# A pooled-attention and gated-convolution kernel rewritten: loads of q, token order and the order of work

## The chip, the cores and the metric

The kernel runs on one core of a Trainium2 chip. The metric is the device time of one execution in microseconds (us). The core has five engines that run in order, each its own list: PE (matmul), DVE (vector), ACT (scalar), POOL (GpSimd, which here issues all casting loads) and SP (SyncE, which here issues stores and DMA transposes). They meet through semaphores. Matmul results lie in PSUM, all else in SBUF.

## The reference

Eight batches, eight heads, 576 tokens, head width 64. Keys and values are averaged over groups of eight tokens; attention runs over these 72; its output goes through a gated block.

```python
k_p = k.reshape(B, H, 72, 8, D).mean(axis=3)      # v_p the same
scores = scale * np.matmul(q, k_p.transpose(0, 1, 3, 2))
attn = softmax(scores)
x = matmul(attn, v_p)                            # [B, 576, heads * 64 = 512]
h = np.maximum(x @ w_in, 0.0)                     # 512 -> 1024
conv_out = sum over k in 0..2 of conv_w[k] * h shifted by k-1 tokens
gate = 1 / (1 + exp(-conv_out))
return (h * gate) @ w_out                          # 1024 -> 512
```

q, k, v are normal draws times 0.1, all in float32; the kernel works in bfloat16 with float32 sums.

## The kernel before, in words

Each piece of work is an operation with a name, an engine, inputs and outputs. A list scheduler in the kernel (`Planner`, numbers in `PARAMS["prio"]`) puts them in one order when the program is built; each engine gets its part of it. Where a copy may run on two engines, `PARAMS["act"]` lists the names that go to ACT and the rest go to DVE. Filler matmuls on a tile of zeros (L388) are put where the scheduler expects PE to wait in its first 60 us.

Per batch b the work is:

- `ldk`, `ldv`, `ldq`: loads by POOL, cast to bf16 (L447, L451, L467, L479, L424, L412). All go through POOL's one in-order list.
- Pooling of k and v: three adds on DVE (L605, L612, then L622 for `ksum` or L654 for `vs`). `kT` transposes `ksum` on PE, `kz` copies it into a zero-padded tile.
- q for batches 0 to 4: loaded as [72 rows, heads, 8 tokens x 64], two buffers `q_b`; `qg` regroups it on DVE or ACT into `q2` (L432); 32 PE transposes of 72 columns (`qT`, L688) and copies `qTe` (L694) bring it to `qT`. Its tokens are then in an order of (token mod 8, row). q for batches 5 to 7: five loads of rows of 64 elements (L412) and five DMA transposes by SP (L676) from the same buffer.
- `sc` (scores, L717 and L719): five blocks, each 512 and 64 columns; `exp` on ACT (L725) writes `attnT`. `av` (L742, L746) gives the output and the row sums for 128 tokens (64 for the last tile); `rc` and `nm` on DVE (L755, L759) normalise into `xx`.
- `xt`: `xx` is transposed to `xT` on PE against a permutation matrix `perm` that puts the tokens back in order (L779, copy L785), or by DMA for batches 5 to 7 (L772).
- `mm1` (L799 in two token parts for batch 0, L822 for the others) and `relu` on ACT (L806, L828) give `hT`, eight blocks of 128 channels.
- The convolution: for the (batch, block) pairs in `PARAMS["off"]` two scaled copies (`cp0`, `cp2`, L868 on ACT, L870 on DVE) and two adds (`ca0`, `ca2`, L877, L887) on DVE; for the others six matmuls on PE against diagonal matrices `dw` (`conv`, L945), which POOL builds (L571). `off` holds 54 of 64.
- The gate on ACT (`tanh`, L895 or L952): a sigmoid, or a tanh whose half-plus-half step `tg1` then runs on DVE (L923). A sigmoid needs another function table than exp: a table load before it and one back. Then `g` on DVE (L933) multiplies by h into `gT`.
- `mm2` (L976) per pair of batches, nine row tiles of 128, copies `oe` (L999, L989) and stores by SP (L1004, L994).

w_in is one casting load of 1 MB out of 2 MB (L485), w_out two.

```python
QG = {True: [(0, 8), (8, 16), (16, 24), (24, 32)], False: [(0, 11), (11, 22), (22, 32)]}
"rg": "DDDDDTTT",     # D: regroup and PE transposes; T: small rows and DMA transposes
```

Of the kernel before, what the change touches and what calls it, by code (L numbers as in the profile page):

```python
# [1098 lines left out]
```

## Time and profile before

| | |
|---|---|
| runs, us | 202.21, 202.72, 206.47; median 202.72 |
| profiled execution: span, us | 205.9 |
| PE, DVE, ACT, POOL busy | 95%, 84%, 80%, 28% of the span |
| mean granted TensorE clock | 0.990 |
| DMA: packets, MB | 52,330, 30.02 |

The profiled execution has no other time than its span, the time from its first to its last instruction; it is a separate execution from the three runs. PE's busy share counts filler matmuls (239 of 1770). Engines are listed with the line of the kernel and the tile written and read; a group's mean is the length of one instruction from start to end, which overlaps with the next on the same engine by some 0.1 us. POOL and SP mostly issue transfers, and a transfer's own time is in the DMA rows.

### The profile page before, as it was taken

How to read it: one execution, taken by the hardware profiler on the slowest of the kernel's cores; microseconds unless marked ns; L12 is line 12 of the kernel's file. 1: busy time of each engine (PE TensorE's matmuls, PEld its weight loads, DVE VectorE, ACT ScalarE, POOL GpSimd, SP SyncE). 2: the span in 40 equal slices, each digit the busy share in tenths (PEclk: the TensorE clock that was granted, in tenths of full speed). 3: DMA queues.
4: the chain of work that ended last, by engine and by line, in shares of the span. 5: the costliest groups of instructions: out<-in, count | busy, mean ns of one | idle time of the engine just before them, and what ended most of it. 6: DMA issues, size and time to landing. Idle time of an engine off the chain costs nothing.

```text
span 205.9 us, 4566 instructions
## 1 busy us (share of the span) xinstructions
PE 194.9 (95%) x1770; PEld 133.0 (65%) x1770; DVE 173.3 (84%) x396; ACT 165.3 (80%) x275; POOL 57.0 (28%) x90
## 2 busy tenths in 40 slices
PE   6999999999999999999999999669999999999992
PEld 6978775977557776567755775226756765765541
DVE  3598599999999999999999996893897999778522
ACT  2045799999999999999999999494899867979610
POOL 7999497160223276215412000000000000000000
PEclk9999999999999999999999999996999999999999
DMA  3999999999999999999999999772122625004334
GB/s 32 192 202 205 196 200 200 201 184 192 157 193 238 171 125 173 181 147 158 193 137 167 152 103 151 115 203 105 20 57 41 229 78 155 13 0 168 126 117 154
DMA packets 52330, 30.02 MB, mean 146 GB/s; under 512 B 33468, under 2 KB 47316, under 8 KB 52308
## 3 DMA queue, kind: packets, MB, share of 16 engines
q0 software_dynamic: 32384, 16.73, 71.8%
q1 hardware_dynamic: 19924, 12.99, 30.5%
q8 instruction: 14, 0.23, 0.6%
q14 instruction: 8, 0.07, 0.2%
HBM read 33.44 MB, written 9.44 MB: 208 GB/s over the span
## 4 chain that ended last, share of the span: by engine, by line
PE 38%; DMA 26%; ACT 16%; DVE 12%; issue 3%; POOL 3%; SPq 0%; POOLq 0%; DVEq 0%; ACTq 0%
PE psfB L976 14%; DMA v_b<-in_v_dram 13%; PE psfA L822 12%; DMA q_b<-in_q_dram 6%; DMA qT<-q 6%; ACT tg L895 4%; PE pswA L388 3%; ACT attnT L725 3%; PE psfA L742 2%; ACT hT L828 2%; ACT cv L868 2%; PE psfA L945 2%; DVE p L605 2%; DVE cv L870 1%; DMA xT<-xx 1%
## 5 line engine op out<-in xcount | busy, mean ns | idle before, releaser
L976 PE MATMUL psfB<-w_out,gT 128*128 128x512 bf16 (+1 forms) x282 | 65.4, 378 | 0.0
L822 PE MATMUL psfA<-xT,w_in 128*128 128x288 bf16 x448 | 60.0, 291 | 2.2 <-DMA xT<-xx 2.2
L822 PEld LDWEIGHTS <-w_in 128*128 128x128 bf16 x448 | 43.9, 100 | 16.2 <-DMA xT<-xx 2.4
L976 PEld LDWEIGHTS <-gT 128*128 128x128 bf16 x290 | 27.3, 98 | 28.9
L828 ACT ACTIVATE hT<-psfA 128x576 bf16<-128x576 f32 x56 | 35.1, 656 | 8.4 <-PE psfA L822 8.2
L870 DVE TENSOR_SCALAR cv<-hT,cr 128x576 bf16<-128x576 bf16 x75 | 26.3, 378 | 5.6 <-ACT hT L828 5.4
L933 DVE TENSOR_TENSOR gT<-tg,hT 128x1152 bf16<-128x1152 bf16 x32 | 23.6, 749 | 3.9 <-ACT tg L895 2.0
L759 DVE TENSOR_TENSOR xx<-psfA,rr 128x512 bf16<-128x512 f32 (+1 forms) x40 | 26.5, 679 | 0.2
L868 ACT ACTIVATE cv<-hT,cr 128x576 bf16<-128x576 bf16 x33 | 25.1, 776 | 0.4 <-DVE cv L887 0.2
L725 ACT ACTIVATE attnT<-psfA 128x576 bf16<-128x576 f32 x40 | 24.5, 661 | 0.7 <-PE psfA L717 0.5
L895 ACT ACTIVATE tg<-cv,cn 128x576 bf16<-128x576 bf16 x30 | 22.5, 780 | 0.0
L877 DVE TENSOR_TENSOR cv<-cv,hT 128x1152 bf16<-128x1152 bf16 (+1 forms) x31 | 20.9, 676 | 0.3
L887 DVE TENSOR_TENSOR cv<-cv 128x1152 bf16<-128x1152 bf16 (+1 forms) x31 | 20.8, 674 | 0.2
L999 ACT COPY osb<-psfB 128x512 f32<-128x512 f32 x24 | 14.1, 587 | 6.4 <-PE psfB L976 6.3
L412 POOL DMA_DIRECT2D q<-in_q_dram x15 | 12.8, 863 | 20.1 <-DMA qT<-q 11.3
L895 ACT ACTIVATE tg<-cv,cs 128x576 bf16<-128x576 bf16 x24 | 18.2, 772 | 0.2
L388 PEld LDWEIGHTS <-zero 128*128 128x128 bf16 x239 | 16.1, 108 | 2.8 <-DVE zero L497 2.0
L742 PE MATMUL psfA<-vblk,attnT 128*128 128x130 bf16 (+1 forms) x160 | 15.6, 222 | 2.1 <-DVE xx L759 2.0
L742 PEld LDWEIGHTS <-attnT 128*128 128x128 bf16 (+1 forms) x160 | 11.1, 100 | 5.7 <-DVE xx L759 2.9
L388 PE MATMUL pswA<-zero 128*128 128x128 bf16 x150 | 11.5, 249 | 2.0 <-DVE zero L497 2.0
L717 PE MATMUL psfA<-qT,kz 128*128 128x512 bf16 x64 | 12.4, 286 | 0.3
L746 PE MATMUL psfA<-vblk,attnT 128*128 128x130 bf16 (+1 forms) x80 | 11.2, 221 | 0.0
(92 smaller groups left out, 256.6 us busy)
## 6 DMA issues: line engine op xcount, KB each, us to landing
out_dram<-osb SPq DMA_DIRECT2D x14, 512.0 KB, 4.2
k_b<-in_k_dram POOLq DMA_DIRECT2D x8, 512.0 KB, 13.5
v_b<-in_v_dram POOLq DMA_DIRECT2D x7, 512.0 KB, 13.0
q_b<-in_q_dram POOLq DMA_DIRECT2D x4, 576.0 KB, 15.6
out_dram<-osb SPq DMA_DIRECT2D x7, 256.0 KB, 2.2
q<-in_q_dram POOLq DMA_DIRECT2D x12, 128.0 KB, 15.9
w_in<-in_moe_w_in_dram POOLq DMA_DIRECT2D x1, 1024.0 KB, 10.4
w_out<-in_moe_w_out_dram POOLq DMA_DIRECT2D x2, 512.0 KB, 12.5
```

The lines of the kernel that those rows point to most:

```text
L388: nc.tensor.matmul(out=t, lhsT=zero[:, 0:P], rhs=zero[:, 0:P], start=True, stop=True)
L725: nc.scalar.activation(out=attnT[m][:, t, :], in_=slot(key).rearrange("p i x -> p (i x)")[:, 0:S], func=ACT.Exp, scale=1.0 / 64.0)
L742: nc.tensor.matmul(out=a[0:n, g, c * w:(c + 2) * w], lhsT=attnT[m][:, s, u0:u0 + n], rhs=vblk[m][:, 2 * s:2 * s + 2, :].rearrange("p x d - ...
L759: nc.vector.tensor_tensor(out=xx[i3][0:n].rearrange("p (g h e) -> p g h e", g=2, h=4), in0=av_view()[:, :, :, 0:D], in1=rr[i3][0:n].rearra ...
L822: nc.tensor.matmul(out=t[:, i, 0:HC], lhsT=w_in[:, c, f * P:(f + 1) * P], rhs=xT[m][:, c, i * HC:(i + 1) * HC], start=(c == 0), stop=(c == ...
L828: nc.scalar.activation(out=h_(b)[:, f, hs(b), 2:S + 2].rearrange("p (i x) -> p i x", i=2), in_=slot(key)[:, :, 0:HC], func=ACT.Relu)
L868: nc.scalar.activation(out=cv[y][:, kk // 2, z0:z1, :], in_=src, func=ACT.Copy, scale=sc)
L870: nc.vector.tensor_scalar(out=cv[y][:, kk // 2, z0:z1, :], in0=src, scalar1=sc, scalar2=None, op0=OP.mult)
L877: nc.vector.tensor_tensor(out=cv[y][:, 0, 0:n, :], in0=cv[y][:, 0, 0:n, :], in1=h_at(2), op=OP.add)
L895: nc.scalar.activation(out=tg[i3][:, zs[z0]:zs[z0] + z1 - z0, :], in_=cv[y][:, 0, z0:z1, :], func=ACT.Tanh if half else ACT.Sigmoid, scale ...
L933: nc.vector.tensor_tensor(out=o_, in0=tg[i3], in1=h2, op=OP.mult)
L976: nc.tensor.matmul(out=a[:, 0, j0:j1], lhsT=g[:, c, t * P:(t + 1) * P], rhs=w_out[:, c, j0:j1], start=(c == 0), stop=(c == n_fb - 1), skip ...
```

## The change

The kernel is written anew in these parts; the mathematics stays.

- The scheduler is gone. `PARAMS["order"]` lists all operations in one order, with the PSUM slot of each and the fillers (`14A0/77@B1` means 14 fillers in slot A0 ahead of operation 77).
- q is loaded for every batch as [96 rows, 8 heads, 6 tokens x 64], one buffer `q_b` (batch 0 in rows 0 to 64 and 64 to 96). Batches 0 and 1 (`qp`) skip the regrouping: PE transposes each 64-wide half head by head, 48 instructions (96 for batch 0, in two row ranges). Batches 2 to 4 regroup into one of two `q2` and take 24 transposes of 96 columns. Batches 5 to 7 regroup and take two DMA transposes each.
- Batch 0's scores and exps are in two token ranges, 384 and 192.
- exp writes `attnT` in token order, reading PSUM in steps; `xt` transposes against the identity, and `perm` is gone.
- The last tiles of `av`, `nm` and `xt` are 128 rows high; `attnT` has 64 spare columns of ones.
- Half of w_in comes over SP as float32 into `wf`, SP's first instruction, and four copies `wc` cast it (one on ACT, three on DVE); the other half is cast by POOL's DMA.
- k and v of batch 1 are pooled by eight matmuls each (`pmk`, `pmv`); the other batches pool in place.
- `dw` is built on ACT and DVE. `off` holds 57 of 64: PE keeps blocks 1, 3, 5, 7 of batch 0 and 2, 4, 6 of batch 7.
- All gates are tanh, so all 32 pairs have the `tg1` step, and exp and tanh share one table.

```diff
-        for x, (r0, r1) in enumerate(((0, 64), (64, PR)) if PARAMS["qs"][b] else ((0, PR),)):
-                nc.gpsimd.dma_start(out=q_b[b % NQ][r0:r1].rearrange("p h i d -> p h (i d)"), in_=rows_q(b)[r0:r1])
+            nc.gpsimd.dma_start(out=q_b[b % NQ], in_=q[b].rearrange("h (p i) d -> p h (i d)", i=TQ))
...
-                    nc.sync.dma_start(out=flat_q(m)[:, :, P * t:P * t + n], in_=q_rows(b % NQ)[0:n, t], transpose=True)
+                    nc.sync.dma_start(out=flat_out[:, 1152 * j:1152 * j + 1152].rearrange("p (g r) -> p g r", r=PQ), in_=flat_in[:, 1536 * j:1536 * j + 1536], transpose=True)
...
+                        for z in range(2):
+                            nc.tensor.transpose(out=t[64 * z:64 * z + 64, 0, j * PQ:(j + 1) * PQ], in_=q_b[b % NQ][:, 2 * c + z, i * D:(i + 1) * D], identity=ident[0:PQ, 0:PQ])
...
-            nc.scalar.activation(out=attnT[m][:, t, :], in_=slot(key).rearrange("p i x -> p (i x)")[:, 0:S], func=ACT.Exp, scale=1.0 / 64.0)
+            nc.scalar.activation(out=at(m)[:, t, :].rearrange("p (r i j) -> p r i j", i=2, j=3),
+                                 in_=slot(key)[:, :, 0:HC].rearrange("p i (j r) -> p r i j", j=3), func=ACT.Exp, scale=1.0 / 64.0)
...
-                nc.tensor.transpose(out=a[:, 0, c * P:c * P + n], in_=xx[i3][0:n, c * P:(c + 1) * P], identity=(ident[0:n, 0:n] if tr else perm4 if last else perm))
+                nc.tensor.transpose(out=a[:, 0, c * P:(c + 1) * P], in_=xx[i3][:, c * P:(c + 1) * P], identity=ident)
...
+                nc.sync.dma_start(out=wf, in_=moe_w_in.rearrange("(c p) f -> p c f", p=P)[:, :, 0:512])
+                    copy_on(e)(out=w_in[:, c, 0:512], in_=wf[:, c, :])
...
+                for i in range(8):
+                    nc.tensor.matmul(out=t, lhsT=ident, rhs=src[:, :, i * D:(i + 1) * D], start=i == 0, stop=i == 7)
...
-                    nc.gpsimd.tensor_scalar(out=dw[f][:, kk, :], in0=ident, scalar1=s, scalar2=1.0, op0=OP.mult, op1=OP.mult)
+                    if e == "ACT":
+                        nc.scalar.activation(out=dw[f][:, kk, :], in_=ident, func=ACT.Copy, scale=s)
+                    else:
+                        nc.vector.tensor_scalar(out=dw[f][:, kk, :], in0=ident, scalar1=s, scalar2=None, op0=OP.mult)
...
-    "off": [(0, 2, 3, 6, 7), (0, 3, 4, 6, 7), (0, 1, 2, 3, 5, 6, 7), (0, 1, 2, 3, 4, 5, 6, 7), (0, 1, 2, 3, 4, 5, 6, 7), (0, 1, 2, 3, 4, 5, 6, 7), (0, 1, 2, 3, 4, 5, 6, 7), (0, 1, 3, 5, 7)],
-    "sw": [0, 1, 0, 0, 1, 0, 0, 1],
+    "off": [[0, 2, 4, 6], [0, 1, 2, 3, 4, 5, 6, 7], [0, 1, 2, 3, 4, 5, 6, 7], [0, 1, 2, 3, 4, 5, 6, 7], [0, 1, 2, 3, 4, 5, 6, 7], [0, 1, 2, 3, 4, 5, 6, 7], [0, 1, 2, 3, 4, 5, 6, 7], [0, 1, 3, 5, 7]],
```

The new order on POOL begins with the last part of k, 32 rows of q, k, pieces of v and of the next k, then 64 rows of q; the second batch's k is pooled on PE ahead of the first `mm1`.

More of the change, by code (lines that the diff above doesn't have):

```diff
@@ L286, in packets @@
-def packets(n, nbytes, cast=True, engines=16):
-    return n / engines, 0.003 + 0.0000785 * nbytes if cast else 0.004 + 0.000034 * nbytes, engines // 4
+        out, seen = [], set()
+        for x in PARAMS["order"].split():
+            warm = None
+            if "/" in x:
+                w, x = x.split("/")
+                warm = (int(w[:-2]), w[-2:])
+            mode = x.endswith("s")
+            x, _, slot = x.rstrip("s").partition("@")
+            o = self.ops[int(x)]
+            o.mode = mode
+            assert o.i not in seen and seen.issuperset(o.deps) and (o.after is None or o.after in seen), o.name
+            seen.add(o.i)
+            if slot:
+                self.held[o.take] = (slot[0], int(slot[1]))
+            e = next(iter(o.eng)) if len(o.eng) == 1 else "ACT" if o.name in self.on_act else "DVE"
+            out.append((e, o, warm))
@@ L290 @@
+        assert len(out) == len(self.ops)
+        return out
 @with_exitstack
@@ L438, in load_k, with regroup, fn @@
+    def regroup(b):
+        if QP[b]:
+            return
+        for j in range(2):
+            def fn(e, j=j):
+                copy_on(e)(out=q2[b % NR][:, 3 * j:3 * j + 3], in_=q_b[b % NQ][:, :, 192 * j:192 * j + 192].rearrange("p h (i d) -> p i h d", d=D))
+            pl.add(f"qg.{b}.{j}", {"DVE": 0.48, "ACT": 1.37}, 0, fn, reads=[("ql", b % NQ, 0), ("ql", b % NQ, 1)], writes=[("q2", b % NR, j)])
+    def load_k(b):
         m = b % 2
         src = rows(k, b)
-        acc = PARAMS["acc"][b]
@@ L783, in fn @@
+        pl.add(f"xt.{b}.{t}", "PE", 0.222, fn, reads=[("xx", i3), "ident"], writes=[("xtp", b, t)], take=key2, free=[("xT", m, t)])
         def fn(e):
-            w = 64 if last else P
-            copy_on(e)(out=xT[m][:, :, 128 * t:128 * t + w],
-                       in_=slot(key2)[:, 0, 0:512].rearrange("p (c a) -> p c a", c=4)[:, :, 0:w])
-        pl.add(f"xte.{b}.{t}", {"ACT": 0.48, "DVE": 0.335} if not last else {"ACT": 0.265, "DVE": 0.205}, 0, fn, reads=[("xtp", b, t)], writes=[("xT", m, t)],
-               prio=pr + 0.3, give=key2)
```

824 lines of the change are left out of this document (335 added, 489 removed), and 116 rows, old and new, of the table PARAMS.

## The prediction

> **What bounds the kernel now.** I read the page first (shares and slices), then the busy time by stage, then the chain that ended last, and at its longest transfers the timelines of PE, VectorE and GpSimd.
>
> ```profile
> span 205.9 us, 4566 instructions
> PE 194.9 (95%) x1770; PEld 133.0 (65%) x1770; DVE 173.3 (84%) x396; ACT 165.3 (80%) x275; POOL 57.0 (28%) x90
> PEclk9999999999999999999999999996999999999999
> 0.00:5.00 5.00, 3.00 (x29) 3.00 (x30) 1.76 (x7) 1.28 (x1) 3.78 (x10) 1.00 0.35 28
> 5.00:22.24 17.24, 16.91 (x264) 15.01 (x263) 14.06 (x38) 6.11 (x11) 16.48 (x34) 1.00 1.20 200
> 22.24:44.08 21.84, 21.22 (x274) 16.45 (x271) 19.43 (x48) 20.21 (x39) 11.98 (x17) 1.00 1.26 197
> 44.08:120.00 75.92, 75.75 (x683) 51.34 (x681) 74.43 (x172) 74.87 (x125) 24.79 (x32) 1.00 1.60 169
> 120.00:139.22 19.22, 15.01 (x116) 8.16 (x114) 16.47 (x38) 16.09 (x29) 0.00 (x0) 1.00 1.05 146
> 139.22:202.30 63.08, 63.01 (x419) 39.03 (x419) 46.69 (x96) 46.40 (x74) 0.00 (x0) 0.97 0.30 94
> ```
>
> The columns of a stage are its length, then the busy time of PE, weight loads, DVE, ACT and POOL, the granted clock, the DMA share and GB/s. Five stages differ. To 22.24 us PE waits for batch 0 (much of its busy time there is filler matmuls on `zero`), while from 5 us on the DMA moves 200 GB/s without a pause. From 22.24 to 44.08 batch 1's attention still leaves gaps. From 44.08 to 120 PE, DVE and ACT are all full: 75.75, 74.43 and 74.87 of 75.92 us. From 120 to 139.22 PE idles 19.22 - 15.01 = 4.2 us. Behind it PE alone is full. So the page's 95% hides a start, a stage with three bounds, one stall, and a tail that PE sets.
>
> The stall:
>
> ```profile
> 108.03 0.71 POOL L479 DMA_DIRECT2D v_b<-in_v_dram  x1 [1.92 <-DMA q<-in_q_dram]
> 108.03 21.40 DMA v_b<-in_v_dram
> 129.53 0.83 DVE L605 TENSOR_TENSOR p<-v_b 128x1280 bf16<-128x1280 bf16 x1 [2.50 <-DMA v_b<-in_v_dram]
> 131.36 0.42 PE L742 MATMUL psfA<-vblk,attnT 128*64 128x130 bf16 x4 [2.02 <-DVE xx L759]
> 120.25 1.14 PE L822 MATMUL psfA<-xT,w_in 128*128 128x288 bf16 x8
> 121.23 1.89 PE L976 MATMUL psfB<-w_out,gT 128*128 128x512 bf16 x8
> 139.22 6.62 PE L822 MATMUL psfA<-xT,w_in 128*128 128x288 bf16 x39 [2.19 <-DMA xT<-xx]
> 145.68 0.40 PE L742 MATMUL psfA<-vblk,attnT 128*128 128x130 bf16 x4
> ```
>
> The last tail of v is issued at 108.03 behind loads of q and lands 21.4 us later; DVE, in order, sits before it to 129.53, so batch 5's normalisation, its DMA transposes and mm1 of batch 5 are late. After the gap the clock is low: 39 matmuls take 145.68 - 139.22 = 6.46 us, where 8 take 121.23 - 120.25 = 0.98, so 39 take 4.78. That is 1.7 us more. The stall costs 4.2 + 1.7 = 5.9 us.
>
> **The change part by part.**
>
> *Loads of q.* Batches 5 to 7 take q by 15 loads of 64-element rows and 15 DMA transposes; afterwards every batch has one load of 96 rows (six tokens, 384 elements each; batch 0 has two) and batches 5 to 7 two transposes each.
>
> ```profile
> q0 software_dynamic: 32384, 16.73, 71.8%
> DMA packets 52330, 30.02 MB, mean 146 GB/s; under 512 B 33468, under 2 KB 47316, under 8 KB 52308
> L412 POOL DMA_DIRECT2D q<-in_q_dram x15 | 12.8, 863 | 20.1 <-DMA qT<-q 11.3 <-PE psbB L688 4.4 <-DMA q<-in_q_dram 3.8
> q<-in_q_dram POOLq DMA_DIRECT2D x12, 128.0 KB, 15.9
> ```
>
> One batch had 8 x 576 rows, 4608 small packets; three batches make 13,824 of the 33,468 under 512 B. They become 3 x 768 larger ones. POOL loses 12 issues (nine q issues against 21) and the 20.1 us in which it stood before those loads, eleven of them because the q buffer was still being transposed. Its in-order queue then reaches the last v far sooner than 108.03. I take the whole stall away: -5.9 us. Bounds: 0 if another load is as late (q_b is now single, so each q load waits until the one before is regrouped, and k and v loads stand behind it), -5.9 if none is.
>
> *Start.* Half of w_in goes over SyncE as the first transfer; q of batch 0 goes to PE without VectorE's regrouping; scores and exp come in two token ranges (384 and 192).
>
> ```profile
> 8.79 0.84 DVE L605 TENSOR_TENSOR p<-k_b 128x1280 bf16<-128x1280 bf16 x1 [0.16 <-DMA k_b<-in_k_dram]
> 11.78 0.80 ACT L642 COPY kz<-psbB 64x288 bf16<-64x288 bf16 x2 [7.42 <-PE psbB L636]
> 14.68 2.98 ACT L725 ACTIVATE attnT<-psfA 128x576 bf16<-128x576 f32 x5 [0.48 <-PE psfA L717]
> 17.88 0.40 PE L742 MATMUL psfA<-vblk,attnT 128*128 128x130 bf16 x4
> 22.24 0.81 PE L799 MATMUL psfB<-xT,w_in 128*128 128x384 bf16 x4
> L806 ACT ACTIVATE hT<-psfA 128x384 bf16<-128x384 f32 x5 | 2.5, 492 | 0.4 <-PE psfA L799 0.2
> L806 ACT ACTIVATE hT<-psfA 128x192 bf16<-128x192 f32 x3 | 1.0, 332 | 0.0
> L694 ACT COPY qT<-psbB 128x792 bf16<-128x792 bf16 x4 | 3.3, 814 | 0.0
> ```
>
> K is summed from 8.79 and kz is ready at 12.58. 32 rows of q now go ahead of k instead of 8; that is 0.13 MB more in bf16, 0.65 us at 200 GB/s, so kz is ready at about 13.1 us. Then ACT has four short exps, one copy of q and five long ones. Five exps of 576 took 2.98 us, one lasts 0.66, so they follow each other every 0.58; 0.11 us off each mean above for that overlap gives 4 x 0.22 + 0.70 + 5 x 0.38 = 3.5 us, and AV starts at 16.6 instead of 17.88. From there to mm1 I keep the 22.24 - 17.88 = 4.36 us (three normalisations in order on DVE), giving 21.0: -1.3 us. Best case -3 (k not held up, shorter copies). Worst case +1.5: if the half of w_in (1 MB read, as much as a casting load of 0.52 MB reads, so 2.6 us at 200 GB/s) came wholly ahead of k, the chain would be 2.6 us later, 23.6. The PE list has batch 1's k sum (`pmk.1`, eight matmuls of 320 columns, between eight of 288, 0.98 us, and eight of 512) ahead of the first mm1; that k is behind k, q, v and another k, 2.9 MB of bf16 with itself, 14.5 us from 5 us on, so 19.5 us, and about 1.1 us of matmuls end at 20.6, just inside 21.0.
>
> The first half of w_in is cheap because of the row of the first 5 us: 28 GB/s there against 200 later, so 1 MB put there displaces little. The Trainium skill (DMA: Bandwidth & Descriptors, section "Issuing engines are not separate DMA queues") says that transfers issued from different engines share the same DMA engines, and that this saves issue time alone. By that rule alone the start would be the worst case above, +1.5, and the time 2.8 us longer, 199.3, still in the forecast's own range; that the first 5 us are quiet is why I don't take it, and no run here shows it yet.
>
> *Batch 1 and the PE list.*
>
> ```profile
> L388 PE MATMUL pswB<-zero 128*128 128x128 bf16 x49 | 3.7, 219 | 0.0
> 27.80 0.52 PE L688 MATMUL psbA<-ident,q 72*128 72x72 bf16 x11
> 28.15 0.49 PE L688 MATMUL psbB<-ident,q 72*128 72x72 bf16 x10
> L870 DVE TENSOR_SCALAR cv<-hT,cr 128x576 bf16<-128x576 bf16 x75 | 26.3, 378 | 5.6 <-ACT hT L828 5.4
> L868 ACT ACTIVATE cv<-hT,cr 128x576 bf16<-128x576 bf16 x33 | 25.1, 776 | 0.4 <-DVE cv L887 0.2
> L923 DVE TENSOR_SCALAR tg<-tg 128x1152 bf16<-128x1152 bf16 x11 | 4.9, 446 | 0.4 <-ACT tg L895 0.4
> L923 DVE TENSOR_SCALAR tg<-tg 128x576 bf16<-128x576 bf16 x6 | 1.9, 321 | 0.3 <-ACT tg L952 0.3
> L895 ACT ACT_TABLE_LOAD x3 | 3.8, 1283 | 0.1
> L725 ACT ACT_TABLE_LOAD x2 | 2.6, 1283 | 0.0
> ```
>
> From 34 to 44 us PE ran 49 filler matmuls, 3.7 us. The new list keeps 31 there (13 and 18), about 2.3 us, so 1.4 less; one more convolution (six matmuls at 0.1225 = 0.7) and pmv (1.1) come into that stage, three transposes of q (1.1) leave it: +0.7 + 1.1 - 1.1 - 1.4 = -0.7 us. Bounds: +1.3 if batch 1's 48 half-height transposes do not run in pairs (48 x 0.042 = 2.0 instead of 1.0) and the fillers save nothing; -1.8 if no filler was needed. Later, four convolutions leave PE (10 to 7 in all, one more in batch 0): 4 x 0.74 = 3.0 us off; eleven transposes of 72 columns take 28.15 - 27.80 = 0.35 us, so 32 take 1.0, and 24 of 96 columns take the same if the time goes with the columns; but batch 2's now falls into this part: +1 us. PE -2.0, bounds 0 (DVE and ACT hold it) and -3.
>
> *ACT and DVE.* Without sigmoid five table loads go, 6.4 us of ACT. What comes: every pair now gets the half-plus-half step on DVE, 32 of 1152 columns for 11 and 6 half ones, 32 x 0.446 - 6.8 = +7.5 us; copies scaled on ACT go from 33 to 50, +13.2, on DVE from 75 to 64, -4.2; one more add pair +1.4. ACT takes 12 and DVE 9 of the `dw` builds that POOL made, which lie before 13 us where ACT is idle (6.11 busy of 17.24). Regrouping, pooling in place and copies of q roughly cancel. So ACT has 13.2 - 6.4 = 6.8 us more and DVE 7.5 - 4.2 + 1.4 = 4.7. Batches 1 to 4 and with them about six tenths fall into 44 to 120: 4.1 and 2.8, less the idle 1.05 and 1.5 there, 3.0 and 1.3. The engines work in parallel, so I charge the larger, +3.0 us; 0 if PE stays the bound, +6 if every added microsecond of ACT ends on the path.
>
> *Exp in token order.* It now reads PSUM with a step of 96 elements, three at a time. No row has such a read. Lower bound: the 0.66 us of the row at 14.68. Upper: a second step per element. From 384 to 192 columns the mean falls 492 - 332 = 160 ns, 0.83 ns per element, so 576 x 0.83 = 0.48 us more. I take nothing, since a reciprocal over 8 PSUM values 65 apart costs as little as one over 8 in a row:
>
> ```profile
> L755 DVE RECIPROCAL rr<-psfA 128x8 f32<-128x8 f32 x32 | 5.8, 194 | 1.0 <-PE psfA L746 0.7
> L544 DVE RECIPROCAL cn<-cn 128x8 f32<-128x8 f32 x1 | 0.2, 191 | 0.0
> ```
>
> *Sum*, against the profiled 205.9: -5.9 -1.3 -0.7 -2.0 +3.0 = -6.9, so 199.0 as a span. The runs (202.21, 202.72, 206.47) are 3.2 below the span in the median. If that is one offset, 195.8 comes out; if the shorter runs only had less of the stall, which the change can't save twice, 199.0. A transfer's landing is what differs most easily between executions, but the stall's waits alone would have to shrink from 5.9 to 2.7; I go a quarter of the way from 195.8 to 199.0: **196.5 us**.
>
> **The rivals.**
>
> 1. *DVE and ACT become the bound* (44 to 120 is full already). For: 1.05 and 1.5 us idle. Against: PE's order moves matmuls of mm2 into such gaps. All +6 instead of +3.0, and no gain on PE (+2.0): 196.5 + 5 = 201.5.
> 2. *The stall comes back elsewhere*: single q_b, late v. For: 20.1 us of POOL waits show how an in-order queue passes a late buffer on. Against: 13,824 packets fewer. Without the -5.9 of the stall, but with the half of it that short runs may lack: 196.5 + 4 = 200.5.
> 3. *Slower: exp's strided read costs a second step.* 20 exps of batches 1 to 4 add 20 x 0.48 = 9.6 us to ACT where 1.05 is idle, batch 0 adds 2.4 to the chain at the start; batches 5 to 7 hide in ACT's idle 16.7 us of the tail. 196.5 + 11 = 207.5. It decides from 0.27 us more per exp, 0.93 us mean (then 202.7). Beside it: the Trainium skill (PSUM — Partial Sum Buffer, section "Specifications (TRN2)") says that any non-contiguous pattern slows matmuls significantly, for 8-byte lines; it names matmuls, not ACT's reads, and the two reciprocals do not show it.
>
> **How the numbers follow.** Forecast 0.60, rival 1 0.16, rival 2 0.12, rival 3 0.12. The forecast's own range is 192 to 200: above, 199.0 and a little of the start's bad end; below, the start's good end (-1.7), batch 1's (-1.1) and half of the charge for DVE and ACT (-1.5). For eight in ten it is stretched to **191 to 204**, over rivals 1 and 2, leaving rival 3 out. A change under 2% can't be told from none here: faster means below 198.7, slower above 206.8. Faster: 0.60 x 0.93 + 0.28 x 0.25 = 0.63; slower 0.10, nearly all of rival 3; 0.27 between.
>
> **What would show it.** First mm1 of batch 0 at 20 to 22 us, mm1 of batch 1 before 43. No wait of DVE for v above 1 us, PE idle under 1 us between 120 and 140, clock 9 in all later slices. Loads of q landing in under 10 us. ACT exps of 576 near 660 ns: above 900 rival 3 is right. DVE and ACT over 98% busy with PE idle between 44 and 120: rival 1. A DVE or PE wait of some us for DMA anywhere: rival 2. The forecast is wrong if mm1 starts after 23 us or PE idles more than 5 us behind 44.

## The result: 5.9% slower, and where the time went

| | before | after |
|---|---|---|
| time, us, median | 202.53 | 213.72 (213.12 to 214.95) |
| span of the profiled execution, us | 205.9 | 211.9 |
| ratio after to before, 95% interval | | 1.0585 (1.0517 to 1.0654) |

The forecast was 196.5. In every run of this study that has both numbers the time is the span plus 1.66 to 1.89 us, so the profiled 205.9 of the kernel before stands for some 207.6: it was one of its long executions, 5 us above the median. A second profiled execution of the same kernel had a span of 201.8 and a time of 203.47. The comparisons below go against that one, called the ordinary execution. The ratios compare only executions within 1.5% of the fastest of their kernel: the kernel before also has longer ones, of 204 to 208 us, and where it was run beside the kernel with direct transposes (below) they were 8 of 13, so that over all executions the direct transposes' median, 206.18, is 0.9% above the median of before, 204.43, and not the 1.8% of its ratio.

The page of the kernel after, and its busy time in four of the stages that the prediction used (length, then PE, weight loads, DVE, ACT, POOL, clock, DMA share, GB/s):

```profile
span 211.9 us, 4546 instructions
PE 192.2 (91%) x1752; PEld 130.9 (62%) x1767; DVE 177.7 (84%) x407; ACT 174.4 (82%) x307; POOL 37.4 (18%) x65
PEclk9999999999999999999997599999999999999999
```

```profile
0.00:5.00 5.00, 3.00 (x31) 3.00 (x32) 1.76 (x7) 1.28 (x1) 3.89 (x11) 1.00 0.54 180
5.00:22.24 17.24, 13.07 (x262) 11.14 (x260) 10.74 (x40) 9.84 (x27) 13.14 (x27) 1.00 1.19 183
...
44.08:120.00 75.92, 67.49 (x584) 44.82 (x587) 70.08 (x150) 66.96 (x115) 13.29 (x18) 0.96 1.07 158
120.00:139.22 19.22, 18.43 (x168) 13.03 (x169) 18.34 (x44) 18.38 (x32) 0.00 (x0) 0.98 0.58 129
```

The stall of the stage from 120 us is gone, as forecast: PE is idle for 0.8 us there. But the stage ahead of it, which had 0.2 us idle, now has 8.4, with the clock at 0.96 and a dip to 5 tenths in the page's row. Two of the prediction's own signs of being wrong are there: more than 5 us of idle PE behind 44, and a first mm1 after 23 us (24.92, below). To see how far each kernel is at a given time, take the first relu of a batch as a milestone. First the kernel after, then the ordinary execution of the kernel before, both from the timeline of ACT, for batches 1, 3 and 4:

```profile
47.47 0.63 ACT L709 ACTIVATE hT<-psfA 128x576 bf16<-128x576 f32 x1
99.84 0.65 ACT L709 ACTIVATE hT<-psfA 128x576 bf16<-128x576 f32 x1
128.53 0.64 ACT L709 ACTIVATE hT<-psfA 128x576 bf16<-128x576 f32 x1
```

```profile
45.76 0.67 ACT L828 ACTIVATE hT<-psfA 128x576 bf16<-128x576 f32 x1
95.00 0.65 ACT L828 ACTIVATE hT<-psfA 128x576 bf16<-128x576 f32 x1
114.57 0.65 ACT L828 ACTIVATE hT<-psfA 128x576 bf16<-128x576 f32 x1
```

The differences of these starts, and the rest up to the end of the span, give a table that all experiments are read by:

| profiled execution | to batch 1 | 1 to 3 | 3 to 4 | 4 to end | span |
|---|---|---|---|---|---|
| before, ordinary | 45.76 | 49.24 | 19.57 | 87.23 | 201.8 |
| after | 47.47 | 52.37 | 28.69 | 83.37 | 211.9 |
| two q buffers | 48.84 | 52.40 | 24.67 | 83.09 | 209.0 |
| and later v sum | 48.72 | 52.39 | 21.79 | 83.30 | 206.2 |
| and direct q for batches 2 to 4 | 47.00 | 50.91 | 21.83 | 83.36 | 203.1 |

After against before: +1.7, +3.1, +9.1 and -3.9 us. The largest loss, in the third column, is a wait. The kernel after from 97 to 116 us, from the timelines of POOL, SP, DVE, ACT and PE:

```profile
97.55 0.94 DVE L269 COPY q<-q_b 96x1536 bf16<-96x1536 bf16 x1
...
98.56 15.56 SPq L544 DMA_TRANSPOSE qT<-q  x2
...
98.79 0.78 POOL L261 DMA_DIRECT2D q_b<-in_q_dram  x1 [0.15 <-issue]
...
111.81 0.95 DVE L269 COPY q<-q_b 96x1536 bf16<-96x1536 bf16 x1 [4.13 <-DMA q_b<-in_q_dram]
...
111.85 1.47 ACT L269 COPY q<-q_b 96x1536 bf16<-96x1536 bf16 x1 [5.09 <-issue]
...
113.41 0.40 PE L659 MATMUL psbA<-ident,xx 128*128 128x128 bf16 x4 [3.58 <-DVE xx L641]
115.18 3.57 PE L838 MATMUL psfB<-w_out,gT 128*128 128x512 bf16 x8 [1.38 <-ACT osb L861]
```

Batch 5's last regrouping frees the only q_b at 98.49 and POOL issues batch 6's load at 98.79. In the same moment SP starts the two DMA transposes of batch 5's q, and the load is usable 13 us later. The regrouping of batch 6 stands in the middle of batch 4's normalisation on DVE and of the convolution copies on ACT, so both stop, PE idles 3.58 and 1.38 us, and then eight matmuls of 512 columns take 3.57 us instead of 1.89 (the granted clock from 115 to 119 us is 0.50).

The start, from the timelines of PE and DVE, then the load of k and the DMA rate from the view of the DMA queues over the first 12 us (40 slices of 0.3 us):

```profile
8.76 0.93 PE L532 MATMUL psbB<-ident,q_b 32*64 32x32 bf16 x48 [2.46 <-DMA q_b<-in_q_dram]
...
11.34 0.82 DVE L421 TENSOR_TENSOR k_b<-k_b 128x1280 bf16<-128x1280 bf16 x1
...
24.92 1.46 PE L688 MATMUL psfB<-xT,w_in 128*128 128x384 bf16 x8
```

```profile
GB/s 0 0 0 0 0 0 55 0 7 225 403 389 410 423 416 389 410 379 226 196 197 177 163 149 166 202 182 109 102 116 147 198 195 196 185 201 195 206 202 205
...
k_b<-in_k_dram POOLq DMA_DIRECT2D x1, 512.0 KB, 8.7
```

The last line gives the 512 KB of k 8.7 us from its issue, at 2.57, to its landing. From 3.0 to 5.4 us the DMA moves about 400 GB/s, which is the half of w_in; q is there at 8.76 and k's first sum starts at 11.34 instead of 8.79.

### The profile page after: what moved, and what is told of

Same layout as the page of the kernel before. It is cut to its first block, busy times and chain, and to the rows that moved or that the text cites. A ratio compares the mean times of both kernels' runs of the same rounds, so it can differ in the third digit from the quotient of the medians.

```text
span 211.9 us, 4546 instructions
## 1 busy us (share of the span) xinstructions
PE 192.2 (91%) x1752; PEld 130.9 (62%) x1767; DVE 177.7 (84%) x407; ACT 174.4 (82%) x307; POOL 37.4 (18%) x65
## 2 busy tenths in 40 slices
DMA packets 40987, 30.55 MB, mean 144 GB/s; under 512 B 18348, under 2 KB 35972, under 8 KB 40964
## 4 chain that ended last, share of the span: by engine, by line
PE 57%; DVE 16%; issue 13%; DMA 7%; ACT 3%; POOL 2%; ACTq 0%; POOLq 0%
PE psfB L838 20%; PE psfA L703 15%; DMA q_b<-in_q_dram 7%; PE pswA L237 3%; PE psfB L688 3%; PE psfA L624 3%; PE psfA L808 3%; DVE xx L641 2%; PE psfA L598 2%; PE psbB L659 2%; DVE q L269 1%; ACT attnT L587 1%; DVE cv L746 1%; PE psfA L628 1%; DVE cv L739 1%
## 5 line engine op out<-in xcount | busy, mean ns | idle before, releaser
L759 ACT ACTIVATE tg<-cv,cs 128x576 bf16<-128x576 bf16 x57 | 43.4, 789 | 1.5 <-DVE cv L751 1.5
L737 ACT ACTIVATE cv<-hT,cr 128x576 bf16<-128x576 bf16 x50 | 38.5, 787 | 0.2
L641 DVE TENSOR_TENSOR xx<-psfA,rr 128x512 bf16<-128x512 f32 x40 | 26.8, 683 | 0.2
L751 DVE TENSOR_TENSOR cv<-cv 128x1152 bf16<-128x1152 bf16 (+1 forms) x32 | 21.6, 683 | 1.8 <-ACT cv L737 1.5
L739 DVE TENSOR_SCALAR cv<-hT,cr 128x576 bf16<-128x576 bf16 x64 | 22.3, 365 | 0.3
L786 DVE TENSOR_SCALAR tg<-tg 128x1152 bf16<-128x1152 bf16 x32 | 14.5, 459 | 3.5 <-ACT tg L814 2.5
L624 PE MATMUL psfA<-vblk,attnT 128*128 128x130 bf16 x160 | 15.9, 221 | 1.7 <-ACT attnT L587 1.2
L624 PEld LDWEIGHTS <-attnT 128*128 128x128 bf16 x160 | 11.9, 98 | 5.0 <-issue 1.2
L269 DVE COPY q<-q_b 96x1536 bf16<-96x1536 bf16 x11 | 10.2, 933 | 4.1 <-DMA q_b<-in_q_dram 4.1
L237 PEld LDWEIGHTS <-zero 128*128 128x128 bf16 x182 | 11.8, 105 | 2.0 <-DVE zero L325 2.0
L237 PE MATMUL pswA<-zero 128*128 128x128 bf16 x159 | 11.2, 234 | 2.0 <-DVE zero L325 2.0
L598 PE MATMUL psfA<-qT,kz 128*128 128x288 bf16 x56 | 11.2, 297 | 0.8 <-DVE xx L641 0.4
L628 PE MATMUL psfA<-vblk,attnT 128*128 128x130 bf16 x80 | 11.2, 221 | 0.0
```

What stands on the lines that cost most here:

```text
L237: nc.tensor.matmul(out=t, lhsT=zero[:, 0:P], rhs=zero[:, 0:P], start=True, stop=True)
L624: nc.tensor.matmul(out=a[:, g, c * w:(c + 2) * w], lhsT=attnT[m][:, S * s + u0:S * s + u0 + P], rhs=vblk[m][:, 2 * s:2 * s + 2, :].rearran ...
L641: nc.vector.tensor_tensor(out=xx[i3].rearrange("p (g h e) -> p g h e", g=2, h=4), in0=av_view()[:, :, :, 0:D], in1=rr[i3].rearrange("p (g ...
L737: nc.scalar.activation(out=cv[y][:, kk // 2, z0:z1, :], in_=src, func=ACT.Copy, scale=sc)
L739: nc.vector.tensor_scalar(out=cv[y][:, kk // 2, z0:z1, :], in0=src, scalar1=sc, scalar2=None, op0=OP.mult)
L759: nc.scalar.activation(out=tg[i3][:, zs[z0]:zs[z0] + z1 - z0, :], in_=cv[y][:, 0, z0:z1, :], func=ACT.Tanh if half else ACT.Sigmoid, scale ...
```

## The experiments

In the diffs the order is written with the operations' names; the kernel's list has numbers. Ratios are to the kernel before on the same chip.

### Two buffers of q, and the sum of v

```diff
-    "nq": 1,
+    "nq": 2,
-  ldq5 ldv7.t ldq6 ldv7.0 ldq7          (POOL)
+  ldq5 ldq6 ldv7.t ldv7.0 ldq7
```

> Two buffers q_b instead of one, and the load of batch 6's q stands ahead of the last part of batch 7's v in GpSimd's list; else as after the change. Theory A (the single buffer makes the stall: batch 6's q may be loaded only when batch 5's is regrouped): the load is issued near 84 us instead of 98.79, no wait of VectorE or ScalarE for q_b above 0.5 us, PE idle between 100 and 120 falls from 5.0 us to under 1, the granted clock stays 1.00 there; time 213.7 - 6 = 207.7 (206 to 209). Rival B (the two transposes of q of batch 5 crowd the DMA engines, whatever the buffer): another transfer is late in its place, time 212 to 214.

Measured 210.88, ratio 1.0348 (1.0239 to 1.0457). The load of batch 6's q is issued at 84.95, and neither DVE nor ACT waits for q_b any more. But part of the stall stays (stage from 100 to 120 us, then DVE and PE in it, then two DMA issues between 99 and 100.7 us with their time to landing):

```profile
100.00:120.00 20.00, 17.51 (x133) 11.83 (x134) 17.66 (x40) 16.55 (x28) 1.60 (x3) 0.91 1.26 151
```

```profile
113.77 0.83 DVE L423 TENSOR_TENSOR v_b<-v_b 128x1280 bf16<-128x1280 bf16 x1 [1.44 <-DMA v_b<-in_v_dram]
...
115.50 0.40 PE L661 MATMUL psbB<-ident,xx 128*128 128x128 bf16 x4 [2.24 <-DVE xx L643]
```

```profile
v_b<-in_v_dram POOLq DMA_DIRECT2D x1, 512.0 KB, 13.6
v_b<-in_v_dram POOLq DMA_DIRECT2D x1, 128.0 KB, 7.4
```

Both theories had a part: the single buffer cost 4.0 us (28.69 to 24.67), and another transfer was late in its place. It is the 512 KB of batch 7's v, issued at 100.03, landed 13.6 us later and summed at 113.77; the last 128 KB of that v, issued just ahead of it at 99.33, had landed 7 us before. In the kernel after, the same 512 KB land no earlier, at 113.9, but DVE, held up by q, comes to them only at 115.06. Nothing needs that sum so early. So it was moved, on top of the two buffers:

```diff
-  cp0.3.7 vp1.7 rc.4.3 rc.4.2 nm.4.3 ... vp2.7     (DVE)
+  cp0.3.7 rc.4.3 rc.4.2 nm.4.3 ... vp1.7 vp2.7
```

> The two-buffer kernel, and the first sum of batch 7's v (vp1.7) stands on VectorE just ahead of its second instead of inside batch 4's normalisation. Theory A (VectorE's wait for the last part of that v, 1.44 us at 113.77, and the half clock behind it are what is left of the stall): PE idle between 100 and 120 falls from 2.5 us to under 0.5, clock 1.00 there, time 210.9 - 3 = 208 (206.5 to 209.5). Rival B (VectorE is full there and the next late thing takes its place): within 1 us of 210.9.

Measured 207.43, ratio 1.0200 (1.0135 to 1.0266):

```profile
100.00:120.00 20.00, 18.83 (x157) 12.57 (x159) 19.92 (x44) 19.78 (x34) 1.47 (x2) 1.00 1.31 131
```

DVE and ACT are full and the clock is whole; PE idles 1.2 us, nearly all of it one wait for a DMA transpose of q. The step from batch 3 to 4 is 2.9 us shorter again. Together the two edits took 6.9 us out of that step and 6.3 out of the time. The second edit alone, with one buffer:

> The kernel after the change with one buffer of q, and only the first sum of batch 7's v moved later. Theory A (the two faults of the order stand one behind the other, the single buffer first): VectorE's and ScalarE's waits for q_b to 111.8 us stay, time within 1.5 us of 213.7. Rival B (the early sum of v is the whole stall): PE idle between 100 and 120 under 1.5 us, time 208 to 209.

Measured 215.00, ratio 1.0569 (1.0472 to 1.0665): the waits for q_b stay (4.9 us of DVE, 5.9 of ACT, against 4.1 and 5.1 in the kernel after), and there is no gain. The faults stand one behind the other, and the first hides the second.

### The kernel before once more

> The kernel before, unchanged, for a second profiled execution. Theory A (the stall behind 120 us is in some executions only, so its 5.9 us were not there to be saved in the median): PE idle between 120 and 140 under 1.5 us, the last v lands in under 14 us, span 200 to 202. Rival B (it is in all of them): PE idle there 3 us or more, span 204 to 206.

Span 201.8, time 203.47. Its stages, then the last load of v and PE's one wait between 115 and 142 us, from the timelines of POOL, DVE and PE:

```profile
44.08:120.00 75.92, 75.32 (x675) 51.34 (x680) 74.45 (x172) 74.71 (x124) 25.25 (x33) 1.00 1.68 182
120.00:139.22 19.22, 17.08 (x132) 9.91 (x132) 16.62 (x38) 16.86 (x30) 0.00 (x0) 1.00 0.88 163
```

```profile
105.63 0.72 POOL L479 DMA_DIRECT2D v_b<-in_v_dram  x1
...
127.06 0.83 DVE L605 TENSOR_TENSOR p<-v_b 128x1280 bf16<-128x1280 bf16 x1 [0.26 <-DMA v_b<-in_v_dram]
...
136.75 4.95 PE L822 MATMUL psfA<-xT,w_in 128*128 128x288 bf16 x39 [2.04 <-DMA xT<-xx]
```

The load takes 21.3 us here too (so "under 14 us" was wrong), but it was issued 2.4 us earlier and DVE comes to it just in time. What is left is 2.1 us of idle PE at full clock (over the 1.5 of theory A), against the 5.9 that the prediction read off the other execution. The two executions are together up to batch 4's first relu (114.57 and 114.79); 3.9 of the 4.1 us between their spans lie behind it. Theory A holds for the time: in this execution, the only ordinary one with a profile, the stall is worth 2.1 us.

And that rest is not the late v. The prediction's 4.2 us of idle PE were two waits, 2.02 us for DVE behind the late v and 2.19 us for the DMA transposes into `xT`, and it took the second for a consequence of the first. Here the first is gone and the second is still there, 2.04 us.

### The start

Half of w_in over SyncE, but later:

```diff
+            def go(e):
+                nc.vector.memset(wf[:, 0, 0:2], 0.0)
+            pl.add("wfgo", "DVE", 0.1, go, writes=["wf"])
-  ldwf ldcw                                  (SP)
+  ldcw ldwf
```

> The half of w_in that goes over SyncE starts only when cw is ready (SyncE waits for a memset of two columns of wf on VectorE), and its four casts stand behind the attention of batch 0; else as after the change. Theory A (that 1 MB comes ahead of k and q): k's first sum starts at 8.8 to 9.5 us instead of 11.34, the first mm1 of batch 0 at 22 to 23 instead of 25.09, time 2 to 3 us shorter, 211. Rival B (the transposes of q head by head and the two token ranges set the start): the first mm1 stays above 24.3, time within 1 us of 213.7.

Measured 215.41, ratio 1.0582 (1.0477 to 1.0688). k's sum starts at 10.63, but now batch 0's v is late: DVE waits 4.3 us for it, and the first mm1 is at 26.82. Both theories missed the time: the 1 MB had only been put in front of another load.

> The edits of the two-buffer kernel and of the late wf together. Theory A (the two losses stand one behind the other): the gains add, 213.7 - 6 - 2.5 = 205.2 (203.5 to 207). Rival B (VectorE's full stretch between 48 and 107 us swallows what the start gives): no better than two buffers alone by 1 us, 207 to 209 or more.

Measured 211.68, ratio 1.0415 (1.0326 to 1.0503), with the first mm1 at 27.74: no better than two buffers alone, as rival B had it, though by the late v and not by DVE.

The half of w_in by POOL behind v, on the kernel with two buffers and the later v sum:

```diff
-    "wf": 1,
+    "wf": 0,
-  ldv0.0 ldk2.0 ldk1.0 ... ldwi1             (POOL)
+  ldv0.0 ldwi0 ldk1.0 ldk2.0 ... ldwi1
```

> The kernel with the later v sum, and the half of w_in comes as a casting load by GpSimd right behind batch 0's v (no wf, no casts), batch 1's k behind it. Theory A (the early 1 MB over SyncE holds up k and q): first sum of k before 9.8 us, first mm1 of batch 0 at 22 to 23.5 us, time 2 to 3 us below the kernel with the later v sum, 205.5. Rival B (whatever comes first, the bytes ahead of the first mm1 are the same): first mm1 at 24.5 us or later, within 1 us of it.

Measured 208.41, ratio 1.0224 (1.0127 to 1.0321). k's sum comes at 9.78 and the first mm1 at 23.13, both as theory A had it, but PE then waits 3.0 us for the other half of w_in and batch 1 is no earlier (50.24). The time followed rival B.

Both halves of that list were turned round, with `wf` kept:

```diff
-  ldv0.0 ldk2.0 ldk1.0 ... ldwi1             (POOL)
+  ldv0.0 ldwi1 ldk1.0 ... ldk2.0
-  nm.0.4 kp1.2 kp2.2 xte.0.3 ...             (DVE)
+  nm.0.4 xte.0.3 ... kz.1.0 kz.1.1 kp1.2 kp2.2
```

> The kernel with two buffers and the later v sum, and in GpSimd's list the casting half of w_in and batch 1's k stand ahead of batch 2's k; VectorE sums batch 2's k behind batch 1's kz copies. Theory A (order of the loads): PE's 1.6 us wait for w_in at 29 us goes, the first relu of batch 1 comes at 46 to 47 instead of 48.7, time 207.4 - 2 = 205.4. Rival B (the DMA engines are full from 5 to 44 us, so another load is late by as much): first relu of batch 1 at 48 or later, within 1 us of 207.4.

Measured 208.60, ratio 1.0235 (1.0132 to 1.0338): PE's wait for w_in is gone, the first relu of batch 1 is at 47.70, and the time has not moved, as rival B had it. The next ones carry the direct transposes of the section below.

> The direct transposes of q for batches 2 to 4 and the start order together. Theory A: the gains add, 207.4 - 2.5 - 2 = 202.9, no slower than the kernel before by more than 1%. Rival B: one of them swallows the other, 205 or more.

Measured 207.69, ratio 1.0190 (1.0072 to 1.0308). The gains do not add, which is rival B: from batch 1 to 4 it takes 72.2 us, as short as with the direct transposes alone, but the first relu of batch 1 is at 49.81.

```diff
-  51 fillers, qT.0.1.0, cwT, 71 fillers, kT.0     (PE)
+  51 fillers, cwT, qT.0.1.0, 58 fillers, kT.0
```

> The kernel with both, and at the start cw's transpose stands ahead of q's on PE, with 58 instead of 71 filler matmuls ahead of k's transpose. Theory A (a fixed number of fillers behind a late q holds up k): k's transpose starts as soon as ksum is there, the first AV 0.5 to 1 us earlier, time 0.5 to 1 us shorter. Rival B (the fillers only stand where PE waits anyway, and fewer of them cost clock): no shorter, granted clock below 1.00 between 14 and 26 us.

Measured 206.89, ratio 1.0166 (1.0092 to 1.0241); against the run above the difference is inside the intervals. Then the whole of w_in by POOL, on the kernel with the direct transposes but without these two orders:

```diff
-    "wf": 1,
+    "wf": 0,
-  ldv0.0 ldk2.0 ldk1.0 ... ldwi1             (POOL)
+  ldv0.0 ldwi0 ldwi1 ldk1.0 ldk2.0 ...
```

> The kernel with two buffers, the later v sum and direct transposes of q for batches 2 to 4, and the whole of w_in as two casting loads by GpSimd right behind batch 0's v and ahead of batch 1's k, as the kernel before has it. Theory A (the start is lost to w_in, half of it too early and half too late): no wait of PE for w_in above 0.5 us, first relu of batch 1 at 46 us (47.0 to 48.7 with wf), time 206.2 - 1.5 = 204.7. Rival B (k of batch 1 is then as late, and PE waits for it): first relu of batch 1 at 47.5 or later, time 206 or more.

Measured 209.51, ratio 1.0338 (1.0265 to 1.0411). Rival B, from the timeline of PE:

```profile
24.64 1.35 PE L439 MATMUL psfA<-k_b,ident 128*128 128x320 bf16 x8 [3.03 <-DMA k_b<-in_k_dram]
25.78 2.77 PE L689 MATMUL psfB<-xT,w_in 128*128 128x384 bf16 x8
```

PE came to this point of its list at 21.6; batch 1's k sum, which stands ahead of the first mm1, had no data yet, and after 3 us of idle the first mm1 ran at a granted clock of 0.50 (2.77 us for eight matmuls that take 1.46). So `pmk.1` went behind five mm1, once with w_in by POOL and once with half of it over SyncE; batch 2's k is also summed later in both, which the diff below does not show:

```diff
-  pmk.1 mm1.0.3.0 mm1.0.2.0 ... mm1.0.7.0 mm1.0.4.0        (PE)
+  mm1.0.3.0 mm1.0.2.0 ... mm1.0.7.0 mm1.0.4.0 pmk.1
```

> The kernel with two buffers, the later v sum, direct transposes of q for batches 2 to 4 and w_in by GpSimd, and PE's sum of batch 1's k (pmk.1) stands behind five of batch 0's mm1 instead of ahead of all; batch 2's k is summed later too. Theory A (in the run with w_in by GpSimd the 3.03 us wait for batch 1's k, which stood ahead of the first mm1, ate the gain): first mm1 at 21.5 to 22.5 us instead of 25.78, first relu of batch 1 at 46 to 47 instead of 51.67, time 3 us below that run, 206.5, or 2% above the kernel before. Rival B (k and w_in share the same DMA time, so mm1 waits for w_in instead): first mm1 after 24, no gain.

> The same move of batch 1's and batch 2's k, but half of w_in over SyncE as after the change and the other half ahead of batch 1's k. Theory A (half of w_in over SyncE is worth its place once k of batch 1 does not stand ahead of mm1): first mm1 at 22 to 23, time 1 to 2 us below the kernel with both the direct transposes and the start order, ratio to before 1.01 or less. Rival B: it waits for batch 0's own chain (k held up by wf), first mm1 above 23.5, no gain.

Measured 206.64, ratio 1.0186 (1.0124 to 1.0247) by POOL; 208.65, ratio 1.0257 (1.0176 to 1.0338) over SyncE. The first sum of k on DVE and the first mm1 on PE, in this order of kernels, and the load of k in the first of them:

```profile
9.61 0.81 DVE L422 TENSOR_TENSOR k_b<-k_b 128x1280 bf16<-128x1280 bf16 x1
...
22.10 1.46 PE L689 MATMUL psfB<-xT,w_in 128*128 128x384 bf16 x8 [0.67 <-ACT xT L664]
...
k_b<-in_k_dram POOLq DMA_DIRECT2D x1, 512.0 KB, 6.0
```

```profile
11.50 0.82 DVE L422 TENSOR_TENSOR k_b<-k_b 128x1280 bf16<-128x1280 bf16 x1 [0.44 <-DMA k_b<-in_k_dram]
...
25.33 1.46 PE L689 MATMUL psfB<-xT,w_in 128*128 128x384 bf16 x8 [0.67 <-ACT xT L664]
```

By POOL, theory A holds for the first mm1 and for the time (206.5). Over SyncE it is rival B, no gain. These two differ in w_in alone; with SyncE's half k's sum is 1.9 us later here, the first mm1 3.2 us, and the time 2.0 us, with intervals that overlap. The profiled execution over SyncE was the longest of its four (210.85), with a clock of 0.64 from 10 to 14 us (see the last section), so a part of the 3.2 us is that clock.

How much later k comes is best read from its load. From issue to landing the 512 KB of k take 7.7 to 9.0 us in the twelve profiles with SyncE's half in front (mean 8.3), 6.0 to 7.3 in the four with w_in by POOL alone (mean 6.3; the two with the half behind cw are in neither), and 6.2 and 5.6 in the two of the kernel before, where the issue is also 0.4 us earlier. So SyncE's half costs k some 2.0 us, and the other order of POOL's loads 0.8. k's first sum shows only 1.2 of the 2.0: it starts between 10.54 and 11.71 us in the twelve (mean 11.0) and between 9.61 and 10.29 in the four (mean 9.8), because in those four DVE is still building `dw` when k has landed (in the first kernel above k lands at 8.6 us and the last `dw` ends at 9.7). In the kernel before it starts at 8.26 and 8.79.

The first relu of batch 1 was not at 46 to 47 but at 48.99 by POOL: with mm1 early, PE waits 0.78 us for batch 1's k and 1.35 us for its q.

### The middle

```diff
-            if half:
+            if half and b not in (1, 2, 3, 4):
```

> Leaves out the half-plus-half step of the gate for batches 1 to 4 (16 instructions of VectorE of 459 ns, 6 us beside their overlap), so the gate of these batches is a plain tanh; else as after the change. Theory A (VectorE is the bound between 48 and 107 us): PE's idle time between 50 and 100, 3.4 us, goes, time 3 to 5 us shorter, 209 to 211. Rival B (PE's gaps there come from the order of its list): time within 1 us of 213.7.

Measured 213.15, ratio 1.0468 (1.0355 to 1.0582). The time is within 1 us of the kernel after, as rival B had it. But this profiled execution was the longest of its four, and it lost 3.5 us before batch 1's first relu, at a clock of 0.50 (last section). From batch 1 to 3 it takes 51.58 us instead of 52.37, from 3 to 4 27.48 instead of 28.69: 2.0 us for 6 us of DVE. The kernel after and the seven others that keep the step, these convolutions and the regroupings take 52.37 to 52.40 us from batch 1 to 3, so the 0.8 us there are the edit's. DVE is a bound, but not alone. DVE's and ACT's busy time from the first relu of batch 1 to that of batch 4, and the regrouping in that stretch, in the ordinary execution of before and in the kernel with two buffers and the later v sum:

```profile
45.76:114.57 68.81, 68.21 (x613) 45.71 (x618) 67.34 (x158) 67.60 (x113) 23.74 (x31) 1.00 1.71 186
```

```profile
L432 DVE COPY q<-q_b 72x2048 bf16<-72x2048 bf16 x3 | 2.3, 762 | 0.0
```

```profile
48.72:122.90 74.18, 69.54 (x619) 46.28 (x624) 73.89 (x160) 71.27 (x122) 11.97 (x16) 1.00 1.13 168
```

```profile
L271 DVE COPY q<-q_b 96x1536 bf16<-96x1536 bf16 x11 | 10.2, 932 | 0.0
```

DVE has 6.6 us more. The eight more regroupings alone are 7.9 (other work is less): those of batches 5 to 7, which had none before, fall into this stretch too. So batches 2 to 4 were given the direct transposes:

```diff
-    "qp": [1, 1, 0, 0, 0, 0, 0, 0],
+    "qp": [1, 1, 1, 1, 1, 0, 0, 0],
```

> The kernel with two buffers and the later v sum, and batches 2 to 4 skip the regrouping as batches 0 and 1 do (PE transposes their q head by head from q_b). Theory A (the regroupings, all of them on VectorE between 48 and 107 us, are what makes that stretch long): VectorE loses 6 x 0.93 = 5.6 us there, PE gets some 1.5; from batch 1's first relu to batch 4's 71 us instead of 74.2, time 207.4 - 2.5 = 204.9. Rival B (ScalarE, 71.3 busy of these 74.2 us, and PE's longer transposes hold the end): within 1 us of 207.4.

Measured 206.18 (ten runs), ratio 1.0181 (1.0131 to 1.0231). From batch 1 to 4 it takes 72.7 us: 1.4 of the expected 3.2. ACT is busy 39.87 of 40 us from 60 to 100, so it probably holds the rest. The runs do not resolve the gain: the ratio was 1.0200 (1.0135 to 1.0266) without this edit. Giving the other regroupings to POOL:

```diff
-{"DVE": 0.48, "ACT": 1.37}
+{"POOL": 1.5} if b > 4 else {"DVE": 0.48, "ACT": 1.37}
```

> The kernel with two buffers, the later v sum and direct transposes of q for batches 2 to 4, and GpSimd regroups q of batches 5 to 7, behind its loads. Theory A (what is left in the middle is regrouping on VectorE): VectorE loses 5 x 0.93 and ScalarE 1.5 us between 90 and 130; from batch 3's first relu to batch 5's 39.5 us instead of 40.9, time 206.2 - 1.5 = 204.7. Rival B (a copy of 96 x 1536 on GpSimd takes several us, or slows VectorE's instructions beside it): the transposes of batch 5's q start later than 98 us, or VectorE's means there rise by over 5%; time 206 or more.

Measured 209.51, ratio 1.0386 (1.0331 to 1.0441). Rival B, and strongly (timelines of DVE and POOL):

```profile
99.12 4.42 DVE L797 TENSOR_TENSOR gT<-tg,hT 128x1152 bf16<-128x1152 bf16 x1
...
100.05 2.88 POOL L270 COPY q<-q_b 96x1536 bf16<-96x1536 bf16 x2
```

A product that takes 0.75 us elsewhere stood for 4.42 us, over both of POOL's copies; in the next run it took 4.42 us beside them again. The Trainium skill (SBUF — State Buffer, section "Who interferes with whom") says that a VectorE instruction with two SBUF inputs contends with a GpSimd instruction that reads SBUF, by a lock and not by sharing; this trace agrees.

> Both edits, GpSimd's regrouping and w_in by two casting loads. Theory A: 206.2 - 3 = 203.2, within 1% of the kernel before. Rival B: 206 or more.

Measured 212.31, ratio 1.0487 (1.0425 to 1.0550): rival B, with both losses. Last, four convolutions back to PE, on the kernel with two buffers and the later v sum:

```diff
-    "off": [[0, 2, 4, 6], [0, 1, 2, 3, 4, 5, 6, 7], [0, 1, 2, 3, 4, 5, 6, 7], ...
+    "off": [[0, 2, 4, 6], [0, 2, 3, 4, 6, 7], [0, 2, 3, 4, 6, 7], ...
```

> The kernel with the later v sum, and four convolutions go back from VectorE and ScalarE to PE: blocks 1 and 5 of batches 1 and 2. Theory A (VectorE and ScalarE are the bound between 48 and 107 us, PE has 4 us idle there): VectorE loses about 4 us and ScalarE 2.7, PE gets 2.9 into its gaps; time 2 to 4 us below the kernel with the later v sum, 205 if that is 208. Rival B (PE is the bound, as the prediction's gain of 2.0 us for fewer convolutions has it): 1 to 3 us above it.

Measured 211.77, ratio 1.0380 (1.0287 to 1.0473). That is slower than either theory had it. From batch 1 to 3 it takes 56.1 us in the profiled execution (the longest of its four), yet from 80 to 100 us DVE is busy 16.5 of 20, ACT 16.8 and PE 18.8. No engine was full: the four were put in by hand, ACT stood 2.0 us for PE and DVE 2.6 us for ACT. It does not tell whether PE could have taken them in a better order.

No version is faster than the kernel before; the nearest ones are 1.7 to 1.9% slower.

## Why the prediction was wrong, point by point

| step | predicted, us | measured, us |
|---|---|---|
| offset of runs to the profile | -2.5 | time = span + 1.66 to 1.89 |
| stall of before taken away | -5.9 | -2.1 in the ordinary execution |
| the stall elsewhere (rival 2) | 0 | +6.9 |
| start and batch 1 | -2.0 | +1.7 (+1.2 to +5.2 in the eight profiles with the same start) |
| ACT and DVE in batches 1 to 4 | +3.0 | +5.3 |
| shorter PE list behind them | -2.0 | -1.8 |
| exp in token order | 0 | 0 |

Against the ordinary span the measured terms give 1.7 + 5.3 + 6.9 - 2.1 - 1.8 = 10.0, and 211.9 - 201.8 = 10.1. (5.3 is 3.1 from batch 1 to 3 and 9.1 - 6.9 from 3 to 4; behind batch 4 the kernel gained 3.9, of which before's own stall is 2.1. So 5.3 and 1.8 are what the other terms leave, and that the sum closes proves nothing of itself.)

*The stall.* This is the step that failed most: "I take the whole stall away: -5.9", with 0 as its worst bound. In the ordinary execution only 2.1 us were there, and those were the wait for `xT` and not the late v; and the new order made a stall of its own, 6.9 us. Rival 2 named both causes, "single q_b, late v", and was priced as a gain not made. That is too low: the new stall is longer than the old one. The step asked when POOL's queue reaches each load, and not where each consumer stands. A regrouping placed 9 us behind its load's issue on two in-order engines needs a load that lands in 9 us, beside two DMA transposes that occupy SP for 15.56 us. The packets did fall (under 512 B from 33,468 to 18,348), and the load still took 13 us. That the transposes are why is not shown.

*The offset.* A median 3.2 us below a profiled span should have been read as "this execution is a long one", and the first suspect is the very stall that the change was to save. The prediction saw that ("the shorter runs only had less of the stall") and then went three quarters of the way to the other reading.

*The start.* "The first 5 us are quiet" was the failed reading: the 28 GB/s were a queue that had just begun, not free capacity (in that execution POOL's first load was issued at 1.43 us, and the rate reaches 188 GB/s at 5.1 us). k's first sum came 2.6 us later. That this is the very number of the worst case is chance: by the mean landings 2.0 us are the 1 MB in front and 0.8 the new order of loads, which the step left out. The Trainium skill's rule that was set aside (DMA: Bandwidth & Descriptors, section "Issuing engines are not separate DMA queues") agrees with the trace in this: SyncE's transfer pushed POOL's back, k by those 2.0 us. The 23.6 us that the prediction worked out from it (+1.4 against 22.24, not the +1.5 it has) were still too early: batch 1's k sum started at 23.84 and stood 1.08 us ahead of the first mm1, and the prediction had it done before mm1 could start.

*ACT and DVE.* The term was mis-sized by "regrouping, pooling in place and copies of q roughly cancel". They did not: eleven copies of 0.93 us on DVE against three, all in the full stretch. DVE was to have 2.8 us more between 44 and 120 us, and by the two stretches above it has 6.6 more between batches 1 and 4; ACT was to have 4.1 more and has 3.7. Rival 1 had the mechanism, with 201.5 as its price.

*Right.* The exps of 576 elements read PSUM in steps at no cost, so rival 3 falls. The reason given for it was thin, though: at 0.83 ns per element eight elements differ by 7 ns, and L544 reads SBUF, not PSUM. The gate's step `tg1` and the copies cost what was counted. Groups of the kernel after:

```profile
L737 ACT ACTIVATE cv<-hT,cr 128x576 bf16<-128x576 bf16 x50 | 38.5, 787 | 0.2
L606 ACT ACTIVATE attnT<-psfA 128x576 bf16<-128x576 f32 x35 | 22.0, 665 | 0.5 <-PE psfA L598 0.3
...
L786 DVE TENSOR_SCALAR tg<-tg 128x1152 bf16<-128x1152 bf16 x32 | 14.5, 459 | 3.5 <-ACT tg L814 2.5 <-ACT tg L759 1.0
```

The exps take 665 ns against 661 before. And the shorter PE list gave about its 2.0: behind batch 4's first relu PE is busy 78.8 us against 81.0, and the time there is 1.8 us shorter without before's stall. The two bounds of batch 1 don't follow from their terms (+1.7 and -3.0 come out, not +1.3 and -1.8), which decides nothing here.

*Open.* Of the 11.2 us, 6.3 are shown by edits to be the two faults of the order (by the ratios to the kernel before, 5.9% and 2.0%, some 7.8). For the regrouping of batches 2 to 4 the traces show 1.4 us, and the runs do not resolve it. By the milestones the last 1.7 to 1.9% lie in the start and in ACT and DVE between batches 1 and 4; no edit gave them back, and in the start each move made another load the late one.

## What to carry to other kernels

When a change rewrites the order by hand, price each load by where its consumer stands in an in-order engine, not only by where the issue stands: a copy that waits for data stops everything behind it, and a single buffer ties the next load to it. Count a stall as a gain only after a second profile of the same kernel shows it again. And a transfer put in front of a queue that is about to fill was not free here: name the load that it pushes back.
